# Value rows on every fourth partition, and key transposes that write columns four apart, in a fused attention and feed-forward kernel

## The chip, the cores and the metric

The kernel runs on one core of a Trainium2 chip. The metric is the device time of one execution in microseconds (us); each kernel was run several times, and the median is quoted. The profiled execution has a "span" that is about 2 to 3 us shorter than its time (271.4 us beside times of 274.21 to 275.49 before). PE is the matmul engine, DVE the vector engine, ACT the scalar engine, POOL the general engine (here it casts fp32 to bf16), and SP issues DMA.

## The reference, cut to what matters

```python
def _attn_ref(q, k, v, p):           # q, k, v: (8, 8, 576, 64); p: (8, 8, 32, 64), all * 0.1
    p_packed = sm_attn(p, k, v)      # 32 queries against 576 keys, per batch and head
    return sm_attn(q, p_packed, p_packed)

def _moe_ref(x, w_in, w_out):        # x: the attention output as (4608, 512), w_in: (512, 2048), w_out: (2048, 512)
    h = np.maximum(x @ w_in, 0.0)
    return (h * h) @ w_out
```

The first softmax sums over all 576 keys of a head, so the keys may be handled in any order, as long as a key's score and its value meet on the same partition of the second matmul.

## The kernel before

A key index is `a*18 + j`, with `a` from 0 to 31 and `j` from 0 to 17. Keys are loaded with (head, `a`) on the 128 partitions. The kernel has DVE transpose 32x32 blocks (32 keys by 32 of the head dimension in `tr_k`), so that `kT` holds the head dimension on partitions and keys as columns. A chunk of 128 columns becomes the stationary operand of a score matmul, so **column c of a chunk becomes partition c of the scores**, and the value of that key has to lie on partition c of the value tile. Before, columns run (`jp`, `a`), so a value load with fixed `jp` fills 32 adjacent partitions.

```python
def dma_v(self, i, h0, h1, eng):                       # six loads per batch
    src = v[self.b, h0:h1].rearrange("h (a j) d -> a h j d", j=JT)
    if i < 4:
        eng.dma_start(v_f[32 * i:32 * i + 32, h0:h1, :GM * D].rearrange("p h (g d) -> p h g d", d=D),
                      src[:, :, i * GM:(i + 1) * GM, :])
    else:
        o = 32 * (i - 4)
        eng.dma_start(v_f[o:o + 32, h0:h1, GM * D:], src[:, :, JM + i - 4, :])

def tr_k(self, qd):
    nc.vector.transpose(                               # 1024 elements per partition
        self.kT[:, qd, :, :GM * P].rearrange("p dh (g jp a) -> p jp g dh a", jp=4, a=32), ...)
    nc.vector.transpose(                               # the remaining 64 keys: 128 elements
        self.kT[:, qd, :, GM * P:].rearrange("p dh (j a) -> p j dh a", a=32), ...)

def s1(self, qd):                                      # scores: kT is the stationary operand
    ...
    nc.tensor.matmul(ps[:, g * P:(g + 1) * P], lhsT=self.kT[:, qd, dh, g * P:(g + 1) * P],
                     rhs=pT_bd[self.b % 2][:, ...], start=(dh == 0), stop=(dh == 1))
```

The order of the instructions on each engine is not written by hand. While the kernel is built, a greedy planner places every step on a model time line, with a cost in us for each, and the program is emitted in that order. A cost that is changed changes the order:

```python
def load_step(name, us, fn, slot): ...
load_step(f"Lv.{b}.{p}.{i}", (1.22 if i < 4 else 0.37) / n, ...)   # value loads: 5.6 us a batch
us = 1.45 if nm == "k" else 1.38                                    # key and query transposes
# ... some 20 streams of such steps, then plan.run()
```

The softmax here doesn't subtract the row's maximum and nothing guards it: scores larger than these inputs give would overflow.

Of the kernel before, what the change touches and what calls it, by code (L numbers as in the profile page):

```python
# [9 lines left out]
ACT = mybir.ActivationFunctionType  # L10
ALU = mybir.AluOpType
F32 = mybir.dt.float32
BF16 = mybir.dt.bfloat16

P = 128
D = 64
NP = 32
QH = 4
JT = 18
GM = 4  # L20
REM = 64
FB = 128
WCH = 512

# [262 lines left out]
def kernel_impl(tc, q, k, v, p, w_in, w_out, out):  # L287
    nc = tc.nc
    B, H, S, Dh = q.shape
    assert Dh == D and S == JT * 32 and H == 2 * QH  # L290
    NQD = H // QH
# [6 lines left out]
    JH = JT // 2  # L298
    TOK = B * S
    NW = 6  # L300
    JM = JT // GM * GM
    NT = TOK // P

    with ExitStack() as ctx:
        ctx.enter_context(tc.manual_schedule())
        consts = ctx.enter_context(tc.tile_pool(name="consts", bufs=1))
# [3 lines left out]
        att = ctx.enter_context(tc.tile_pool(name="att", bufs=2))  # L310
# [10 lines left out]
        w_in_b = consts.tile([P, QH, DFF], BF16, name="w_in_b")  # L321
        w_out_b = consts.tile([P, NFB, NE], BF16, name="w_out_b")
        ones_bd = consts.tile([P, P], BF16, name="ones_bd")
        ones_c = consts.tile([P, 2], BF16, name="ones_c")
        e1_r = [consts.tile([P, NQD, P], BF16, name=f"e1_r{i}") for i in range(2)]
        idle_b = consts.tile([P, 256], BF16, name="idle_b")
        v_f = consts.tile([P, H, (GM + 1) * D], F32, name="v_f")
        pT = consts.tile([P, B * NQD, 2, 32], BF16, name="pT")
# [13 lines left out]
                eng.tensor_copy(dst, src)  # L342

        def setup():
            nc.vector.memset(pT_bd[0][:, :512], 0.0)
            nc.vector.memset(ones_c, 8.0)
            nc.vector.memset(ones_c[REM:, 1:2], 0.0)
            for i in range(2):
                nc.gpsimd.memset(e1_r[i][REM:], 0.0)
            nc.vector.memset(v_f[64:128, :, GM * D:], 0.0)  # L350
            for i in range(2):
                nc.gpsimd.memset(pq_bd[i][:, :512], 0.0)
            nc.gpsimd.memset(idle_b, 0.0)
            nc.gpsimd.memset(ones_bd, 0.0)
            for h in range(QH):
                nc.gpsimd.memset(ones_bd[32 * h:32 * h + 32, 32 * h:32 * h + 32], 0.125)
            nc.gpsimd.memset(pT_bd[1][:, :512], 0.0)

        def keep_clock(ps):
            for _ in range(plan.fill):  # L360
                nc.tensor.matmul(ps, lhsT=idle_b[:, :P], rhs=idle_b, start=True, stop=True)
# [23 lines left out]
        class Loads:  # L385
# [9 lines left out]
                getattr(self, name)[qd] = f  # L395

            def dma_v(self, i, h0, h1, eng):
                src = v[self.b, h0:h1].rearrange("h (a j) d -> a h j d", j=JT)
                if i < 4:
                    eng.dma_start(v_f[32 * i:32 * i + 32, h0:h1, :GM * D].rearrange("p h (g d) -> p h g d", d=D),  # L400
                                  src[:, :, i * GM:(i + 1) * GM, :])
                else:
                    o = 32 * (i - 4)
                    eng.dma_start(v_f[o:o + 32, h0:h1, GM * D:], src[:, :, JM + i - 4, :])

            def new_kq(self, name, qd):
                getattr(self, name + "b")[qd] = qkv.tile([P, JT * D], BF16, name=name + "_b", tag="kqb")
# [34 lines left out]
        class Att:  # L442
# [14 lines left out]
                    self.t.qb[qd][:].rearrange("p (j dh dl) -> p j dh dl", dh=2, dl=32))  # L457

            def tr_k(self, qd):
                self.tile_of("kT", att, [P, NQD, 2, S], BF16, bufs=1)  # L460
                nc.vector.transpose(  # L461
                    self.kT[:, qd, :, :GM * P].rearrange("p dh (g jp a) -> p jp g dh a", jp=4, a=32),
                    self.t.kb[qd][:, :JM * D].rearrange("p (jp g dh dl) -> p jp g dh dl", jp=4, dh=2, dl=32))
                nc.vector.transpose(
                    self.kT[:, qd, :, GM * P:].rearrange("p dh (j a) -> p j dh a", a=32),
                    self.t.kb[qd][:, JM * D:].rearrange("p (j dh dl) -> p j dh dl", dh=2, dl=32))

            def s1(self, qd):
                ps = ps_att.tile([P, 512], F32, name="ps_a", tag="a")
                keep_clock(ps[:, :256])  # L470
                for g in range(GM):
                    for dh in range(2):
                        nc.tensor.matmul(ps[:, g * P:(g + 1) * P], lhsT=self.kT[:, qd, dh, g * P:(g + 1) * P],  # L473
                                         rhs=pT_bd[self.b % 2][:, (qd * 2 + dh) * P:(qd * 2 + dh + 1) * P],
                                         start=(dh == 0), stop=(dh == 1))
                self.ps1[qd] = ps
# [5 lines left out]
            def s1_rest(self):  # L482
                ps = ps_att.tile([P, 512], F32, name="ps_a", tag="a")
                keep_clock(ps[:, :256])
                for qd in range(NQD):
                    for dh in range(2):
                        nc.tensor.matmul(ps[:REM, qd * P:(qd + 1) * P], lhsT=self.kT[:, qd, dh, GM * P:],  # L487
                                         rhs=pT_bd[self.b % 2][:, (qd * 2 + dh) * P:(qd * 2 + dh + 1) * P],
                                         start=(dh == 0), stop=(dh == 1))
                self.psr = ps  # L490

            def s1_rest_exp(self):
                nc.scalar.activation(e1_r[self.b % 2][:REM], self.psr[:REM, :NQD * P], ACT.Exp, scale=0.125)

            def pv(self, qd):
                if qd == 0:
                    self.ps_pp = ps_att.tile([P, 512], F32, name="ps_pp", tag="a")
                    keep_clock(self.ps_pp[:, :256])
                ps = self.ps_pp
                def e1(g, i0, i1):  # L500
                    return self.e1[:, qd, g, i0:i1] if g < GM else e1_r[self.b % 2][:, qd, i0:i1]

                for pr in range(2):
                    h0 = qd * QH + 2 * pr
                    c0 = qd * P + pr * 64
                    for g in range(GM + 1):
                        nc.tensor.matmul(ps[:, c0:c0 + 64], lhsT=self.t.v[:, g, h0 * D:(h0 + 2) * D],  # L507
                                         rhs=e1(g, pr * 64, pr * 64 + 64), start=(g == 0), stop=(g == GM))
                for g in range(GM + 1):
                    o = 1 if g == GM else 0  # L510
                    nc.tensor.matmul(ps[:, 256 + qd:257 + qd], lhsT=e1(g, 0, P), rhs=ones_c[:, o:o + 1],  # L511
                                     start=(g == 0), stop=(g == GM))
# [149 lines left out]
        def stage(*pieces):  # L662
            return list(pieces)

        def load_step(name, us, fn, slot):
            return Step(name, [stage([("SP", 0.45, fn)]), stage([("DMA", us, lambda: None)])], (), slot, (), lag=1.4)

        def load_steps(b):
            def kq(nm, qd):
                return load_step(f"L{nm}.{b}.{qd}", 1.5, lambda: L[b].dma_kq(nm, qd), [("kq", 1)])  # L670

            def vv(p, n):
                h0, h1 = p * H // n, (p + 1) * H // n
                return [load_step(f"Lv.{b}.{p}.{i}", (1.22 if i < 4 else 0.37) / n,
                                  lambda i=i: L[b].dma_v(i, h0, h1, nc.sync), [("v", 1)] if p == 0 and i == 0 else [])
                        for i in range(6)]

            if b == 0:
                return [kq("k", 0), kq("k", 1), kq("q", 0)] + vv(0, 2) + vv(1, 2) + [kq("q", 1)]
            return [kq("k", 0), kq("k", 1)] + vv(0, 1) + [kq("q", 0), kq("q", 1)]  # L680
# [16 lines left out]
        def cast_steps(b, nm, engs):  # L697
            res = []
            halves = 2 if b == 0 else 1
            for qd in QDS:  # L700
                if nm == "v":
                    lands = [f"Lv.{b}.{qd if b == 0 else 0}.{j}" for j in range(6)]
                    us, fn, new = 1280 / halves, L[b].cast_v, f"Bv.{b}.0"
                    if qd == 0:
                        res.append(Step(new, [stage([("-", 0.0, L[b].new_v)])], lands, [("vb", 1)]))
                else:
                    lands = [f"L{nm}.{b}.{qd}"]
                    us, new = 1152 / halves, f"B{nm}.{b}.{qd}"
                    res.append(Step(new, [stage([("-", 0.0, lambda qd=qd: L[b].new_kq(nm, qd))])], lands, [("kqb", 1)]))

                    def fn(qd, i, n, e):
                        L[b].cast_kq(nm, qd, i, n, e)

                piece = [cast_alt(us, engs, lambda e, fn=fn, qd=qd, i=i: fn(qd, i, halves, e)) for i in range(halves)]
                give = [("kq", 1, lands[0])] if nm != "v" else [("v", 1, f"Lv.{b}.0.0")] if qd == NQD - 1 else []
                res.append(Step(f"C{nm}.{b}.{qd}", [stage([("-", 0.0, lambda: None)]), piece], [new] + lands, (), give))
            return res
# [121 lines left out]
        for nm in "kvq":  # L839
            plan.stream(5, sum([cast_steps(b, nm, (A, V, Q) if b == 0 else (Q,)) for b in range(B)], []))  # L840
# [53 lines left out]
```

## Time and profile before

| | before |
|---|---|
| time, median of the first three runs | 274.54 us (274.21 to 275.49) |
| PE busy | 243.0 of 271.4 us |
| PE idle before 75 us | 22.3 us |
| key transposes per head group (4 of the 8 heads) | 1235 + 269 ns |
| rate while values are loaded | about 205 GB/s |

From the page of the kernel before: busy us per engine, then busy tenths in 40 slices of 6.8 us; the row PEclk is the clock granted to PE in tenths, DMA the busy share of the DMA engines.

```profile
span 271.4 us, 5108 instructions
...
PE 243.0 (90%) x1840; PEld 135.4 (50%) x1840; DVE 172.7 (64%) x325; ACT 168.6 (62%) x302; POOL 82.7 (30%) x127
...
PE   0436967999989999999999999999999999999992
...
DVE  4756799999949899859768974976266504510000
...
PEclk9999999999999999999999999999999999999997
DMA  7999999999897999807955911111111131113223
```

PE is short of work only in the first slices, while the DMA row is full. Busy us of each engine in three stretches (after the stretch and its length: PE, PE weight loads, DVE, ACT, POOL, then granted clock, DMA share and GB/s):

```profile
core 0: us, PE busy (x) PEld busy (x) DVE busy (x) ACT busy (x) POOL busy (x), PEclk, DMA share, GB/s
0.00:75.00 75.00, 52.69 (x387) 29.03 (x388) 60.83 (x106) 42.17 (x73) 38.42 (x56) 1.00 1.02 300
75.00:100.00 25.00, 24.01 (x237) 13.46 (x236) 19.86 (x40) 17.77 (x37) 18.79 (x39) 1.00 0.94 275
100.00:250.00 150.00, 149.78 (x1148) 85.56 (x1141) 91.99 (x181) 105.76 (x188) 25.47 (x34) 1.00 0.40 107
...
```

PE lacks 75.00 - 52.69 = 22.3 us in the first stretch, 1.0 in the second and nothing worth naming up to 250 us. The chain of waits, followed back from the last instruction (start, duration, what):

```profile
...
3.62 7.74 DMA v_f<-in_v_dram
...
11.37 3.08 DMA v_f<-in_v_dram
...
21.96 10.57 DMA kq_f<-in_k_dram
...
```

It begins with 10.8 us of value loads, and the keys of batch 1 are waited for at 21.96 us. The DMA rate in the first 16 us, in slices of 0.4 us:

```profile
DMA  0000779999999969999999999999999899989997
GB/s 0 0 0 0 127 196 380 390 378 226 440 415 415 369 265 392 415 373 314 179 159 200 244 195 210 228 199 200 205 239 175 135 284 347 346 328 319 238 210 200
```

By 7.2 us, 1.9 MB have come in (keys, queries and packed queries, but for the first few values), from 4 us on mostly at 370 to 440 GB/s. The values follow; from 7.6 to 12.8 us the rate is 135 to 244 GB/s, although the busy row shows 8 or 9. Then the next loads push it up again. The key transposes, in the groups of instructions (busy us and mean ns of one behind the first bar):

```profile
...
L461 DVE STREAM_TRANSPOSE kT<-k_b 128x1024 bf16<-128x1024 bf16 x16 | 19.8, 1235 | 5.7 <-PE ps_a L487 4.8 <-POOL k_b L342 0.6
L464 DVE STREAM_TRANSPOSE kT<-k_b 128x128 bf16<-128x128 bf16 x16 | 4.3, 269 | 0.0
...
```

### The profile page before, as it was taken

What the parts mean: (1) busy time and instruction counts of PE and PEld (TensorE: products, weight loads), DVE (VectorE), ACT (ScalarE), POOL (GpSimd) and SP (SyncE); (2) the same over time, 40 slices, a digit from 0 to 9 for tenths busy, and PEclk for the clock granted to TensorE, in tenths of its full rate; (3) what the DMA queues carried; (4) which work ended last, traced back from release to release, by engine and by line L of the source; (5) the groups of instructions that cost most, each with busy time, mean ns of one, the idle gap of its engine ahead of it and who ended that gap; (6) DMA issues with size and microseconds to landing.
All of it is one profiled execution on the core that took longest, in us unless ns stands there. A gap on an engine that the chain in (4) does not pass through costs nothing.

```text
span 271.4 us, 5108 instructions
## 1 busy us (share of the span) xinstructions
PE 243.0 (90%) x1840; PEld 135.4 (50%) x1840; DVE 172.7 (64%) x325; ACT 168.6 (62%) x302; POOL 82.7 (30%) x127
## 2 busy tenths in 40 slices
PE   0436967999989999999999999999999999999992
PEld 0322443456555544665565466556546646644441
DVE  4756799999949899859768974976266504510000
ACT  3436646867548798788868975976587717821110
POOL 5432338629589381362246213000000000000000
PEclk9999999999999999999999999999999999999997
DMA  7999999999897999807955911111111131113223
GB/s 258 230 310 398 270 319 386 358 261 334 176 291 236 259 330 239 332 1 168 328 173 119 280 41 40 41 39 42 39 41 39 39 77 41 40 50 76 73 74 77
DMA packets 31129, 46.99 MB, mean 173 GB/s; under 512 B 10113, under 2 KB 18305, under 8 KB 31105
## 3 DMA queue, kind: packets, MB, share of 16 engines
q1 hardware_dynamic: 30576, 46.55, 60.5%
q8 instruction: 14, 0.23, 0.4%
q10 hardware_dynamic: 528, 0.13, 0.2%
q14 instruction: 11, 0.08, 0.1%
HBM read 37.22 MB, written 9.44 MB: 172 GB/s over the span
## 4 chain that ended last, share of the span: by engine, by line
PE 60%; DVE 18%; DMA 11%; SPq 4%; ACT 2%; issue 2%; POOL 1%; DVEq 0%; POOLq 0%; ACTq 0%
PE ps_o L636 31%; PE ps_h L612 17%; DVE gT L627 6%; DMA v_f<-in_v_dram 4%; DMA kq_f<-in_k_dram 4%; DMA out_dram<-o_sb 3%; DVE qT L455 3%; PE ps_a L542 3%; PE ps_s L572 3%; SPq L645 3%; PE ps_a L473 2%; DVE a L600 2%; PE ps_pp L507 2%; DVE M L552 2%; ACT o_sb L340 1%
## 5 line engine op out<-in xcount | busy, mean ns | idle before, releaser
L636 PE MATMUL ps_o<-w_out_b,gT 128*128 128x512 bf16 x576 | 147.5, 379 | 0.4 <-DVE w_out_b L342 0.3
L620 ACT ACTIVATE r<-ps_h 128x576 bf16<-128x576 f32 x124 | 78.2, 651 | 26.6 <-PE ps_h L612 18.9
L627 DVE TENSOR_TENSOR gT<-r 128x576 bf16<-128x576 bf16 x128 | 71.1, 580 | 28.6 <-ACT r L620 27.7
L612 PE MATMUL ps_h<-a,M 128*128 128x288 bf16 x512 | 82.1, 292 | 2.2 <-DVE r L622 1.2
L636 PEld LDWEIGHTS <-gT 128*128 128x128 bf16 x576 | 54.6, 98 | 50.2 <-issue 4.4
L612 PEld LDWEIGHTS <-M 128*128 128x128 bf16 x512 | 49.7, 99 | 31.6 <-issue 6.1
L340 ACT COPY o_sb<-ps_o 128x512 f32<-128x512 f32 x29 | 17.0, 585 | 32.5 <-DMA out_dram<-o_sb 25.8
L550 ACT ACTIVATE M<-ps_a,rD 128x512 bf16<-128x512 f32 x39 | 26.4, 686 | 6.2 <-PE ps_a L542 5.8
L342 POOL CAST q_b<-kq_f 128x1152 bf16<-128x1152 f32 (+1 forms) x16 | 19.7, 1244 | 25.5 <-DMA kq_f<-in_q_dram 25.2
L342 POOL CAST v_b<-v_f 128x1280 bf16<-128x1280 f32 (+1 forms) x15 | 18.8, 1279 | 27.1 <-PE ps_pp L511 10.1
L461 DVE STREAM_TRANSPOSE kT<-k_b 128x1024 bf16<-128x1024 bf16 x16 | 19.8, 1235 | 5.7 <-PE ps_a L487 4.8
L342 POOL CAST k_b<-kq_f 128x1152 bf16<-128x1152 f32 (+1 forms) x15 | 17.7, 1180 | 13.5 <-DMA kq_f<-in_k_dram 9.4
L455 DVE STREAM_TRANSPOSE qT<-q_b 128x1152 bf16<-128x1152 bf16 x16 | 21.4, 1358 | 0.4 <-ACT q_b L340 0.4
L552 DVE TENSOR_SCALAR M<-ps_a,rD 128x512 bf16<-128x512 f32 x25 | 18.7, 747 | 4.4 <-PE ps_a L542 4.2
L473 PE MATMUL ps_a<-pT_bd,kT 128*128 128x128 bf16 x128 | 10.0, 230 | 11.0 <-DVE pT_bd L342 8.3
L542 PE MATMUL ps_a<-w_in_b,ppT 64*32 64x512 bf16 x256 | 16.8, 413 | 3.0 <-ACT M L550 1.1
L342 POOL COPY pT_bd<-pT 32x64 bf16<-32x64 bf16 x56 | 13.5, 267 | 10.9 <-PE ps_a L487 8.8
L473 PEld LDWEIGHTS <-kT 128*128 128x128 bf16 x128 | 8.6, 103 | 13.4 <-DVE kT L461 9.2
L579 ACT ACTIVATE e<-ps_s,rD 128x576 bf16<-128x576 f32 x16 | 11.4, 739 | 5.8 <-PE ps_s L572 5.7
L342 DVE CAST pq_bd<-ps_pp 32x64 bf16<-32x64 f32 x32 | 7.0, 218 | 11.2 <-PE ps_pp L511 5.9
L572 PE MATMUL ps_s<-qT,pq_bd 128*128 128x288 bf16 x64 | 11.0, 306 | 3.1 <-ACT pq_bd L340 1.8
L600 DVE TENSOR_TENSOR a<-e,rs 128x576 bf16<-128x576 bf16 x16 | 13.6, 848 | 0.0
(51 smaller groups left out, 145.0 us busy)
## 6 DMA issues: line engine op xcount, KB each, us to landing
kq_f<-in_k_dram SPq DMA_DIRECT2D x16, 576.0 KB, 8.2
kq_f<-in_q_dram SPq DMA_DIRECT2D x16, 576.0 KB, 7.1
out_dram<-o_sb SPq DMA_DIRECT2D x144, 64.0 KB, 1.7
v_f<-in_v_dram SPq DMA_DIRECT2D x28, 256.0 KB, 5.9
w_f<-in_moe_w_in_dram SPq DMA_DIRECT2D x8, 512.0 KB, 8.2
w_f<-in_moe_w_out_dram SPq DMA_DIRECT2D x8, 512.0 KB, 8.4
v_f<-in_v_dram SPq DMA_DIRECT2D x8, 128.0 KB, 6.7
v_f<-in_v_dram SPq DMA_DIRECT2D x14, 64.0 KB, 5.9
```

What stands on the lines that cost most here:

```text
L340: nc.scalar.copy(dst, src)
L342: eng.tensor_copy(dst, src)
L455: nc.vector.transpose(self.qT[:, qd].rearrange("p dh (j a) -> p j dh a", a=32), self.t.qb[qd][:].rearrange("p (j dh dl) -> p j dh dl", dh= ...
L461: nc.vector.transpose(self.kT[:, qd, :, :GM * P].rearrange("p dh (g jp a) -> p jp g dh a", jp=4, a=32), self.t.kb[qd][:, :JM * D].rearrang ...
L473: nc.tensor.matmul(ps[:, g * P:(g + 1) * P], lhsT=self.kT[:, qd, dh, g * P:(g + 1) * P], rhs=pT_bd[self.b % 2][:, (qd * 2 + dh) * P:(qd * ...
L542: nc.tensor.matmul(pss[qd][o:o + 32, :], lhsT=self.ppT[64 * e:64 * e + 64, qd, pr, :], rhs=w_in_b[64 * e:64 * e + 64, qd * 2 + pr, c * WCH ...
L550: nc.scalar.activation(dst, self.psm[c][e], ACT.Copy, scale=self.rD[:, e:e + 1])
L552: nc.vector.tensor_scalar_mul(dst, self.psm[c][e], self.rD[:, e:e + 1])
L612: nc.tensor.matmul(ps[:, c, :HALF], lhsT=a.M[:, qd, fb * FB:(fb + 1) * FB], rhs=a.a2[:, qd, c * HALF:(c + 1) * HALF], start=(qd == 0), sto ...
L620: nc.scalar.activation(dst, src, ACT.Relu)
L627: eng.tensor_tensor(out=gT[:, fb, o:o + S], in0=r, in1=r, op=ALU.mult)
L636: nc.tensor.matmul(po[t], lhsT=gT[:, fb, n0:n0 + P], rhs=w_out_b[:, fb, :], start=(fb == 0), stop=(fb == NFB - 1))
```

## The change

The intent is to load the values faster, by letting each value load of 32 partitions reach over the whole height of the tile; the loads into 32 neighbours came in at 135 to 244 GB/s. Value load `i` now writes partitions `i, i+4, i+8, ...`, so key columns must run (`a`, `jp`) too: a transpose writes its 32 columns four apart. Keys are divided 5, 5, 4, 4 among the four loads, with rows of 1.25 and 1 KB, and the fifth chunk is padded with zeros. The planner is told that a batch of values takes 3.24 us instead of 5.6.

```diff
 def dma_v(self, i, h0, h1, eng):
-    src = v[self.b, h0:h1].rearrange("h (a j) d -> a h j d", j=JT)
-    ... # four loads into v_f[32*i:32*i+32], two of 256-byte rows
+    n = GM + 1 if i < 2 else GM
+    src = v[self.b, h0:h1].rearrange("h (a j) d -> a h (j d)", j=JT)
+    eng.dma_start(v_f[i:P:4, h0:h1, :n * D], src[:, :, J0[i] * D:(J0[i] + n) * D])   # J0 = (0, 5, 10, 14)
 def tr_k(self, qd):
-    ... "p dh (g jp a) -> p jp g dh a" ...
+    for i, n in (0, GM + 1), (2, GM):
+        nc.vector.transpose(
+            kT[:, qd, :, :n * P].rearrange("p dh (g a jp) -> p jp g dh a", jp=4, a=32)[:, i:i + 2], ...)
 # score matmul of the fifth chunk: 128 rows instead of 64 (zeros in kT, v_f and ones_c)
-    return [load_step(..., (1.22 if i < 4 else 0.37) / n, ...) for i in range(6)]
+    return [load_step(..., (0.9 if i < 2 else 0.72) / n, ...) for i in range(4)]
 # cut: memsets of the padding, the exp of the fifth chunk over 128 partitions
```

More of the change, by code (lines that the diff above doesn't have):

```diff
@@ L20 @@
 GM = 4
-REM = 64
+J0 = (0, 5, 10, 14)
 FB = 128
@@ L300, in kernel_impl @@
     NW = 6
-    JM = JT // GM * GM
     NT = TOK // P
@@ L323, in kernel_impl @@
         ones_bd = consts.tile([P, P], BF16, name="ones_bd")
-        ones_c = consts.tile([P, 2], BF16, name="ones_c")
-        e1_r = [consts.tile([P, NQD, P], BF16, name=f"e1_r{i}") for i in range(2)]
+        ones_c = consts.tile([P, 33], BF16, name="ones_c")
+        msk = consts.tile([P, 32], BF16, name="msk")
+        kT = consts.tile([P, NQD, 2, (GM + 1) * P], BF16, name="kT")
         idle_b = consts.tile([P, 256], BF16, name="idle_b")
@@ L344, in setup @@
         def setup():
+            nc.vector.memset(v_f[:, :, GM * D:], 0.0)
             nc.vector.memset(pT_bd[0][:, :512], 0.0)
-            nc.vector.memset(ones_c, 8.0)
-            nc.vector.memset(ones_c[REM:, 1:2], 0.0)
-            for i in range(2):
-                nc.gpsimd.memset(e1_r[i][REM:], 0.0)
-            nc.vector.memset(v_f[64:128, :, GM * D:], 0.0)
+            nc.vector.memset(ones_c[:, :1], 8.0)
+            nc.vector.memset(msk, 0.0)
+            nc.vector.memset(msk[:].rearrange("p (x y) -> p x y", y=4)[:, :, :2], 8.0)
+            nc.vector.transpose(ones_c[:, 1:33], msk)
+            for qd in range(NQD):
+                nc.gpsimd.memset(kT[:, qd, :, GM * P:], 0.0)
             for i in range(2):
@@ L397, in dma_v @@
             def dma_v(self, i, h0, h1, eng):
-                src = v[self.b, h0:h1].rearrange("h (a j) d -> a h j d", j=JT)
-                if i < 4:
-                    eng.dma_start(v_f[32 * i:32 * i + 32, h0:h1, :GM * D].rearrange("p h (g d) -> p h g d", d=D),
-                                  src[:, :, i * GM:(i + 1) * GM, :])
-                else:
-                    o = 32 * (i - 4)
-                    eng.dma_start(v_f[o:o + 32, h0:h1, GM * D:], src[:, :, JM + i - 4, :])
+                n = GM + 1 if i < 2 else GM
+                src = v[self.b, h0:h1].rearrange("h (a j) d -> a h (j d)", j=JT)
+                eng.dma_start(v_f[i:P:4, h0:h1, :n * D], src[:, :, J0[i] * D:(J0[i] + n) * D])
             def new_kq(self, name, qd):
@@ L459, in tr_k @@
             def tr_k(self, qd):
-                self.tile_of("kT", att, [P, NQD, 2, S], BF16, bufs=1)
-                nc.vector.transpose(
-                    self.kT[:, qd, :, :GM * P].rearrange("p dh (g jp a) -> p jp g dh a", jp=4, a=32),
-                    self.t.kb[qd][:, :JM * D].rearrange("p (jp g dh dl) -> p jp g dh dl", jp=4, dh=2, dl=32))
-                nc.vector.transpose(
-                    self.kT[:, qd, :, GM * P:].rearrange("p dh (j a) -> p j dh a", a=32),
-                    self.t.kb[qd][:, JM * D:].rearrange("p (j dh dl) -> p j dh dl", dh=2, dl=32))
+                for i, n in (0, GM + 1), (2, GM):
+                    nc.vector.transpose(
+                        kT[:, qd, :, :n * P].rearrange("p dh (g a jp) -> p jp g dh a", jp=4, a=32)[:, i:i + 2],
+                        self.t.kb[qd][:, J0[i] * D:(J0[i] + 2 * n) * D].rearrange(
+                            "p (jp g dh dl) -> p jp g dh dl", jp=2, dh=2, dl=32))
             def s1(self, qd):
@@ L472, in s1 @@
                     for dh in range(2):
-                        nc.tensor.matmul(ps[:, g * P:(g + 1) * P], lhsT=self.kT[:, qd, dh, g * P:(g + 1) * P],
+                        nc.tensor.matmul(ps[:, g * P:(g + 1) * P], lhsT=kT[:, qd, dh, g * P:(g + 1) * P],
                                          rhs=pT_bd[self.b % 2][:, (qd * 2 + dh) * P:(qd * 2 + dh + 1) * P],
@@ L486, in s1_rest @@
                     for dh in range(2):
-                        nc.tensor.matmul(ps[:REM, qd * P:(qd + 1) * P], lhsT=self.kT[:, qd, dh, GM * P:],
+                        nc.tensor.matmul(ps[:, qd * P:(qd + 1) * P], lhsT=kT[:, qd, dh, GM * P:],
                                          rhs=pT_bd[self.b % 2][:, (qd * 2 + dh) * P:(qd * 2 + dh + 1) * P],
@@ L492, in s1_rest_exp @@
             def s1_rest_exp(self):
-                nc.scalar.activation(e1_r[self.b % 2][:REM], self.psr[:REM, :NQD * P], ACT.Exp, scale=0.125)
+                self.tile_of("e1r", att, [P, NQD, P], BF16)
+                nc.scalar.activation(self.e1r, self.psr[:, :NQD * P], ACT.Exp, scale=0.125)
             def pv(self, qd):
@@ L500, in e1 @@
                 def e1(g, i0, i1):
-                    return self.e1[:, qd, g, i0:i1] if g < GM else e1_r[self.b % 2][:, qd, i0:i1]
+                    return self.e1[:, qd, g, i0:i1] if g < GM else self.e1r[:, qd, i0:i1]
                 for pr in range(2):
@@ L673, in vv @@
                 h0, h1 = p * H // n, (p + 1) * H // n
-                return [load_step(f"Lv.{b}.{p}.{i}", (1.22 if i < 4 else 0.37) / n,
+                return [load_step(f"Lv.{b}.{p}.{i}", (0.9 if i < 2 else 0.72) / n,
                                   lambda i=i: L[b].dma_v(i, h0, h1, nc.sync), [("v", 1)] if p == 0 and i == 0 else [])
-                        for i in range(6)]
+                        for i in range(4)]
             if b == 0:
@@ L701, in cast_steps @@
                 if nm == "v":
-                    lands = [f"Lv.{b}.{qd if b == 0 else 0}.{j}" for j in range(6)]
+                    lands = [f"Lv.{b}.{qd if b == 0 else 0}.{j}" for j in range(4)]
                     us, fn, new = 1280 / halves, L[b].cast_v, f"Bv.{b}.0"
```

## The prediction

> **What bounds the kernel now.** TensorE, once fed. Windows view: PE is idle 28.4 of 271.4 us, 22.3 of that before 75 us, 4.4 in the last output stores. From 100 to 250 us it is always busy, and counting matmuls there at their shortest times (0.216 us for 128x512, 0.122 for 128x288) fills nearly all of it: fixed work. Time can be won only at the start. There the DMA row stands at 90 to 110% until 100 us. The chain of waits starts with 10.8 us of value loads (3.62 to 14.45), then batch 1's keys (21.96 to 32.5), then DVE work (90 to 100% busy from 30 to 75 us).
>
> **The suspected cost: loads into 32 adjacent partitions.** In fine slices of the GB/s row, key/query and weight loads move 380 to 420 GB/s, value loads only 180 to 240: about 7.2 to 12.7 us for batch 0 (1.18 MB), again 30 to 36.5 us for batch 1. [...]
>
> **Removed.** Six value loads per batch become four (batch 0: 12 become 8); 4096 rows of 256 B go. Estimated from those rates, 1.18 MB at 205 GB/s = 5.7 us becomes 3.0 to 3.6 us at 330 to 390: 2 to 2.7 us per batch, about 19 us of DMA time over eight. [...]
>
> **Added.** Key transposes: 1235 + 269 ns become 640 + 512 elements. From these durations, slope 1.08 ns per element and 131 ns fixed, an estimate of 822 + 684 = 1506 ns: unchanged if writing columns 8 bytes apart is free; at half rate 1.2 us more for each of 16. The remainder's scores get 128 rows instead of 64, same matmul count; its exp stays near 374 ns. Setup gains under 1 us, hidden behind the first loads.
>
> **On the critical path.** Batch 0's values land 2 to 2.5 us earlier and carry the start (PV, w_in, batch 1's keys at 32.5) with them. Batches 1 and 2 give 2 to 2.5 us of DMA time each, but DVE is full from 36 to 75 us, so only part returns: earlier w_out for the first ps_o (about 7 us of PE capacity is lost from 30 to 45 us), and batch 2's start at 76 us, whose chain waited on POOL 4.3 us for v_f at 61. From batch 3 on the saving is hidden. Sum: 2.3 + about 1.6 = 3.9 us. The instruction order is replanned with cheaper loads: 1 us either way.
>
> **Predicted: 270.6 us, 8 in 10 within 266.8 to 273.8. Faster by over 2%: 0.28; within 2%: 0.69; slower: 0.03.**
>
> **Signs.** Right: over 320 GB/s during value loads; batch-0 value casts end near 13 us instead of 15.1; the first ps_h matmul near 25 us instead of 27.4; PE idle before 75 us down by 3 to 4 us; transposes of 0.82 and 0.68 us; 100 to 250 us unchanged in shape. Wrong: value rate still near 210; transposes of 1.2 us or more; DVE from 36 to 75 us swallowing all of the shift.
>
> **What would make it wrong.** Above 274: slower strided transposes. Below 267: the load rate, not DVE, governed everything up to 75 us, so that the savings of batches 0 to 2 add up.

The step from 205 to between 330 and 390 GB/s stands as the estimate, beside the 380 to 420 that the other loads moved in the trace of before. The sum came to 2.3 + about 1.6 = 3.9 us, and 274.5 less 3.9 gives the 270.6 predicted.

## The result, and the profile after

The changed kernel takes 287.62 us (median of four runs, 285.49 to 289.06), the kernel before 274.38 us in the runs beside it. The ratio is 1.0512, with a 95% interval of 1.0437 to 1.0587: **5% slower**. A ratio here is from fast runs alone, so it is not quite the ratio of the quoted medians.

The same views of the kernel after:

```profile
span 283.6 us, 5045 instructions
...
PE 242.1 (85%) x1809; PEld 137.9 (49%) x1840; DVE 186.1 (66%) x325; ACT 171.2 (60%) x305; POOL 80.7 (28%) x126
...
PE   0368568948996989998997999899999999999993
...
DVE  4968997998599899789869955985255522520000
...
PEclk9999987997999999999999999999999999999999
DMA  7999999923884929719615711201121112112222
```

```profile
core 0: us, PE busy (x) PEld busy (x) DVE busy (x) ACT busy (x) POOL busy (x), PEclk, DMA share, GB/s
0.00:75.00 75.00, 48.24 (x346) 27.62 (x350) 62.16 (x101) 39.49 (x70) 38.93 (x61) 0.93 0.85 297
75.00:100.00 25.00, 21.73 (x228) 13.63 (x230) 21.45 (x41) 19.10 (x39) 11.67 (x22) 1.00 0.79 259
100.00:250.00 150.00, 143.55 (x1110) 83.72 (x1129) 101.78 (x184) 106.86 (x189) 30.12 (x45) 1.00 0.34 106
...
```

PE idle time before 75 us did not fall; it rose from 22.3 to 26.8 us, and the next stretches lose 3.3 and 6.5 us as well. (Of the 6.5 us, 4.7 are four waits of about 1 us, at 102.5, 128.6, 152.6 and 181.9 us. The rest are gaps shorter than 0.25 us, and may be records that are missing: the page lists 1809 matmuls, but 1840 weight loads.) DVE has 13.4 us more work in all (186.1 against 172.7): by the two pages the key transposes take 19.6 us more (43.7 against 19.8 + 4.3), and the multiplications that write `gT` 4.6 us less (66.5 against 71.1). The clock row dips in slices 6, 7 and 10. The start of the chain of waits:

```profile
...
5.86 2.69 DVE kT L459 x2
...
9.46 1.38 DVE kT L459
...
10.87 1.34 DVE kT L459
...
12.26 1.05 PE ps_a L469 x8
...
```

The value loads have left the chain, as was hoped. Key transposes have taken their place at once: 2.69 + 1.38 + 1.34 us of them before the second score matmuls at 12.26. The DMA rate in the first 16 us:

```profile
DMA  0000598699999989999999999999899999899999
GB/s 0 0 0 0 161 392 323 228 350 264 461 429 403 415 357 415 398 377 369 369 357 364 357 366 360 324 315 333 323 332 289 210 227 225 292 394 410 405 374 384
```

This is the success of the change. The values, from about 6.8 to 10.4 us, come in at 324 to 377 GB/s instead of 135 to 244. The change also makes rows and loads fewer, but packets of the same 1,024 bytes took 83 ns on average in the trace before and 55 ns in the trace after, so the rate does not come from larger rows alone. The first matmul of `ps_h` (the feed-forward part) starts at 24.26 us instead of 27.37. But the lead is gone soon after: the first `ps_o` matmul (the last product of the feed-forward part) starts at 45.14 us (45.33 before), and the scores of batch 2 at 76.07 us (75.79 before). The key transposes:

```profile
...
L459 DVE STREAM_TRANSPOSE kT<-k_b 128x640 bf16<-128x640 bf16 x16 | 25.8, 1611 | 5.2 <-PE ps_a L483 5.0
L459 DVE STREAM_TRANSPOSE kT<-k_b 128x512 bf16<-128x512 bf16 x16 | 21.4, 1336 | 0.0
...
```

They take 1611 + 1336 = 2947 ns in place of 1504 (the records of a pair overlap by about 0.2 us, so that a pair keeps DVE busy for about 2.75 us). And in PE's time line there are idle stretches that the kernel before does not have (the last bracket: us idle, and what ended it):

```profile
...
43.30 0.39 PE L539 MATMUL ps_a<-w_in_b,ppT 64*32 64x512 bf16 x1 [2.71 <-DVE ppT L342]
63.63 0.39 PE L633 MATMUL ps_o<-w_out_b,gT 128*128 128x512 bf16 x1 [3.00 <-DVE gT L624]
...
```

The longest idle stretch of the kernel before between 21 and 110 us is 1.31 us.

### The profile page after: what moved, and what is told of

Same layout as the page of the kernel before. It is cut to its first block, busy times and chain, and to the rows that moved or that the text cites. A ratio compares the mean times of both kernels' runs of the same rounds, so it can differ in the third digit from the quotient of the medians.

```text
span 283.6 us, 5045 instructions
## 1 busy us (share of the span) xinstructions
PE 242.1 (85%) x1809; PEld 137.9 (49%) x1840; DVE 186.1 (66%) x325; ACT 171.2 (60%) x305; POOL 80.7 (28%) x126
## 4 chain that ended last, share of the span: by engine, by line
PE 56%; DVE 21%; ACT 6%; DMA 6%; issue 4%; SPq 3%; POOL 3%; ACTq 0%; POOLq 0%
PE ps_o L633 27%; PE ps_h L609 19%; DVE kT L459 11%; DMA out_dram<-o_sb 4%; SPq L642 3%; PE ps_a L539 3%; PE ps_a L469 2%; ACT o_sb L340 2%; DVE M L549 2%; DVE pq_bd L342 2%; DVE gT L624 1%; DMA w_f<-in_p_dram 1%; ACT r L617 1%; PE ps_s L569 1%; PE ps_pp L504 1%
## 5 line engine op out<-in xcount | busy, mean ns | idle before, releaser
L633 PE MATMUL ps_o<-w_out_b,gT 128*128 128x512 bf16 x545 | 141.0, 382 | 4.9 <-DVE gT L624 3.9
L617 ACT ACTIVATE r<-ps_h 128x576 bf16<-128x576 f32 x126 | 79.8, 651 | 28.8 <-PE ps_h L609 20.8
L624 DVE TENSOR_TENSOR gT<-r 128x576 bf16<-128x576 bf16 x128 | 66.5, 539 | 37.4 <-ACT r L617 36.1
L609 PE MATMUL ps_h<-a,M 128*128 128x288 bf16 x512 | 84.9, 298 | 2.4 <-DVE a L597 1.3
L609 PEld LDWEIGHTS <-M 128*128 128x128 bf16 x512 | 50.9, 101 | 31.6 <-issue 5.2
L459 DVE STREAM_TRANSPOSE kT<-k_b 128x640 bf16<-128x640 bf16 (+1 forms) x32 | 43.7, 1473 | 5.2 <-PE ps_a L483 5.0
L547 ACT ACTIVATE M<-ps_a,rD 128x512 bf16<-128x512 f32 x38 | 25.4, 684 | 9.0 <-PE ps_a L539 8.8
L342 POOL CAST q_b<-kq_f 128x1152 bf16<-128x1152 f32 x14 | 17.9, 1287 | 32.9 <-DMA kq_f<-in_q_dram 20.1
L342 POOL CAST k_b<-kq_f 128x1152 bf16<-128x1152 f32 (+1 forms) x15 | 16.7, 1120 | 18.8 <-DMA kq_f<-in_k_dram 8.0
L476 ACT ACTIVATE e<-ps_a 128x512 bf16<-128x512 f32 x16 | 8.9, 597 | 11.9 <-PE ps_a L469 11.8
L539 PEld LDWEIGHTS <-ppT 64*32 64x32 bf16 x256 | 4.6, 90 | 23.1 <-issue 16.7
```

Source lines behind the costliest of these rows:

```text
L342: eng.tensor_copy(dst, src)
L459: nc.vector.transpose(kT[:, qd, :, :n * P].rearrange("p dh (g a jp) -> p jp g dh a", jp=4, a=32)[:, i:i + 2], self.t.kb[qd][:, J0[i] * D:( ...
L539: nc.tensor.matmul(pss[qd][o:o + 32, :], lhsT=self.ppT[64 * e:64 * e + 64, qd, pr, :], rhs=w_in_b[64 * e:64 * e + 64, qd * 2 + pr, c * WCH ...
L547: nc.scalar.activation(dst, self.psm[c][e], ACT.Copy, scale=self.rD[:, e:e + 1])
L609: nc.tensor.matmul(ps[:, c, :HALF], lhsT=a.M[:, qd, fb * FB:(fb + 1) * FB], rhs=a.a2[:, qd, c * HALF:(c + 1) * HALF], start=(qd == 0), sto ...
L617: nc.scalar.activation(dst, src, ACT.Relu)
```

## The experiments

Three suspects came out of the two traces: the strided transposes (T), the new instruction order (R1), and the fast loads themselves, by contention or by the clock (R2). Some experiments pair keys with the wrong values. They all passed the comparison with the reference, so **that comparison does not see a wrong pairing here**. The inputs are scaled by 0.1, so the softmax is nearly uniform; that this is the reason is argued, not shown.

### 1. Strided transposes alone, in the old order (e2_before_strided)

```diff
-    self.kT[...].rearrange("p dh (g jp a) -> p jp g dh a", jp=4, a=32),
+    self.kT[...].rearrange("p dh (g a jp) -> p jp g dh a", jp=4, a=32),
```

The instruction lists of all engines are the same as before. 

> The kernel before, in its own instruction order, with only the main key transposes (1024 elements) writing columns four apart; wrong result on purpose. Theory T (strided transpose writes are the loss): each such transpose takes about 2.4 us instead of 1.235, 16 times, DVE busy up by about 19 us, and the time rises to 283 to 289 us. Rival R1 (the new instruction order is what costs) and rival R2 (the faster loads collide with something, or the granted clock falls by itself): 274 to 276 us, as before.

Measured: 282.05 us beside 274.98, ratio 1.0253 (1.0209 to 1.0296). The group line:

```profile
...
L461 DVE STREAM_TRANSPOSE kT<-k_b 128x1024 bf16<-128x1024 bf16 x16 | 39.3, 2455 | 5.1 <-PE ps_a L487 4.5 <-POOL k_b L342 0.3
...
```

So T is at work by itself: 1235 ns became 2455, and the run became 2.5% slower, just below the range expected. But 5.1% is not explained by this alone.

### 2. The kernel after with contiguous transposes (e5_after_contiguous)

```diff
-    kT[...].rearrange("p dh (g a jp) -> p jp g dh a", jp=4, a=32)[:, i:i + 2],
+    kT[...].rearrange("p dh (g jp a) -> p jp g dh a", jp=4, a=32)[:, i:i + 2],
```

Same order as after, wrong pairing. 

> The kernel after, same instruction order on all engines, key transposes writing 32 contiguous columns again; wrong result on purpose. Theory T: transposes of about 0.82 and 0.69 us, no clock dip from 30 to 50 us, time 267 to 272 us (the gain that was predicted from the loads). R1 and R2: it stays at 282 to 288 us.

Measured: 278.32 us, ratio 1.0124 (1.0059 to 1.0188). The transposes took 834 + 669 ns, and the time fell by 9 us, yet it stayed above the kernel before, although the loads were fast and the transposes cheap. Neither theory fits alone: T predicted at most 272, R1 and R2 at least 282. Its first two stretches, and idle stretches of PE:

```profile
...
0.00:75.00 75.00, 51.69 (x375) 28.72 (x380) 58.50 (x104) 42.03 (x74) 41.50 (x66) 0.93 0.87 302
75.00:100.00 25.00, 21.11 (x197) 12.95 (x199) 18.45 (x36) 17.06 (x34) 13.29 (x24) 0.86 0.74 262
...
```

```profile
...
37.86 2.08 PE L609 MATMUL ps_h<-a,M 128*128 128x288 bf16 x8 [1.72 <-DVE r L619]
41.82 1.22 PE L539 MATMUL ps_a<-w_in_b,ppT 64*32 64x512 bf16 x8 [1.89 <-DVE ppT L342]
87.33 0.75 PE L539 MATMUL ps_a<-w_in_b,ppT 64*32 64x512 bf16 x8 [2.57 <-DVE gT L624]
...
```

The clock dips and the gaps before 100 us did not go away with the strided writes. The four waits after 100 us did: this trace has no PE gap above 0.25 us from 100 to 250 us.

### 3. The planner told the truth about transposes (e3_after_told)

```diff
-    us = 1.45 if nm == "k" else 1.38
+    us = 2.95 if nm == "k" else 1.38
```

> The kernel after, with the planner told that the key transposes of one group take 2.95 us instead of 1.45, so that it orders the work around them; correct result. If the loss is mostly that the order was planned for the wrong duration (R1): 276 us or less. If it is the DVE time itself (T): 279 to 286 us.

Measured: 277.11 us, ratio 1.0071 (1.0023 to 1.0119). The work is that of the change, the result is correct, and 10 us of the loss are gone; it falls between the two forecasts. The order therefore matters as much as the DVE time does.

### 4. The new load cost in the planner alone (e4_before_plan_only)

```diff
-    load_step(..., (1.22 if i < 4 else 0.37) / n, ...)
+    load_step(..., (0.70 if i < 4 else 0.22) / n, ...)
```

Loads and transposes are those of before. 

> The kernel before with nothing but the planner's cost of value loads lowered to the new total (3.2 us instead of 5.6 per batch); loads and transposes as before, correct result. T: 273 to 277 us, only the noise of another order. R1 (an order planned for faster loads is bad): 280 us or more.

Measured: 280.98 us, ratio 1.0194 (1.0135 to 1.0253). A number in the planner, with no work changed, cost 6 us. R1 is real.

### 5. Fast loads in the old order, without and with strides (e6_order_before_contig, e7_order_before_strided)

To take the order out of the comparison, the planner keeps six value steps at the old costs, and the last two issue nothing. The lists of PE, DVE, ACT and POOL then agree with those of before except for the shapes and the memsets of the change itself.

```diff
 def dma_v(self, i, h0, h1, eng):
+    if i > 3:
+        return
-    load_step(..., (0.9 if i < 2 else 0.72) / n, ...) for i in range(4)
+    load_step(..., (1.22 if i < 4 else 0.37) / n, ...) for i in range(6)
```

e7 is the whole change in this order; e6 has contiguous transposes as well (wrong pairing).

> Fast value loads alone: the four new loads, contiguous transposes, and the instruction order of the kernel before (the planner keeps six load steps at the old costs; the last two issue nothing). Keys and values are paired wrongly on purpose. If the predicted gain from the loads exists (2 to 4 us) and the new order hid it: 270.5 to 273 us. If faster loads gain nothing or collide with other work (R2): 274.5 us or more.

> The whole change, correct, in the instruction order of the kernel before. If the loss of the change is the sum of strided transposes (7.1 us in that order) and of the new order: e6 plus 6 to 8 us, 277 to 281 us. If the order is innocent and the parts only interact: 285 us or more, as after.

Measured for e6: ratio 0.9688 (0.9649 to 0.9728). Its six runs fall into two groups, 265.35 to 266.85 and 269.75 to 271.64; the second lies over 1.5% above the fastest run and is left out of the ratio. All six have a median of 268.3, beside 274.8, a gain of 2.4%; so the gain is 2.4 to 3.1%, by whether the second group counts. For e7: 280.54 us, ratio 1.0222 (1.0193 to 1.0250), all six within 1.5 us. The first two stretches of e6:

```profile
...
0.00:75.00 75.00, 55.20 (x450) 31.71 (x451) 60.62 (x112) 43.99 (x80) 42.55 (x76) 1.00 0.96 338
75.00:100.00 25.00, 25.00 (x225) 13.49 (x223) 23.52 (x45) 20.87 (x40) 15.84 (x21) 1.00 0.82 274
...
```

And the first and third of e7:

```profile
...
0.00:75.00 75.00, 50.05 (x369) 28.08 (x370) 65.54 (x106) 40.91 (x71) 36.55 (x53) 0.98 0.87 303
...
100.00:250.00 150.00, 146.04 (x1139) 84.48 (x1139) 102.71 (x186) 107.75 (x191) 25.87 (x35) 1.00 0.34 105
...
```

In e6 PE lacks 19.8 us in the first stretch instead of 22.3, nothing in the second, and the clock reads 1.00. (Over the whole span idle time falls by 3.9 us; the other 3.7 of the 7.6 us between the two profiled spans are PE busy time, 239.3 against 243.0 us for the same matmuls. Why they took less was not found.) Batch 2's scores start at 70.57 us instead of 75.79. So the fast loads do gain, and more than was forecast; R2 falls. In this order the strides turn a gain of 3.1% into a loss of 2.2%: in e7 PE lacks 25.0 us in the first stretch and 4.0 in the third.

### 6. What a column step costs (e8_strides)

The transpose of 512 elements was given another column step in each pair of batches.

```diff
+    if s == 1:  o = d.rearrange("p dh (jp g a) -> p jp g dh a", jp=4, a=32)[:, 2:4]
+    elif s == 2: o = d.rearrange("p dh (g a jp) -> p jp g dh a", jp=2, a=32)[:, :, 4:8]
+    elif s == 8: ...   # s = 4 in batches 0 and 1 as in the change; 16 in batch 7
```

> The second key transpose (512 elements) with a column step of 4 in batches 0 and 1, 1 in 2 and 3, 2 in 4 and 5, 8 in 6 and 16 in 7; wrong result on purpose, only durations count. Theory S1[...]: 0.67 us at step 1 and the same 1.33 us at 2, 4, 8 and 16. Theory S2[...]: step 2 close to 0.67 us, step 4 1.33, steps 8 and 16 above 1.33.

The single run took 291.06 us, which says nothing here. From DVE's time line, one transpose each of step 1, 2, 8 and 16:

```profile
...
61.74 0.71 DVE L475 STREAM_TRANSPOSE kT<-k_b 128x512 bf16<-128x512 bf16 x1
...
122.98 0.75 DVE L475 STREAM_TRANSPOSE kT<-k_b 128x512 bf16<-128x512 bf16 x1
...
145.72 2.47 DVE L475 STREAM_TRANSPOSE kT<-k_b 128x512 bf16<-128x512 bf16 x1 [1.19 <-PE ps_a L487]
...
177.91 2.37 DVE L475 STREAM_TRANSPOSE kT<-k_b 128x512 bf16<-128x512 bf16 x1 [1.43 <-PE ps_a L487]
...
```

Step 4 took 1.34 us in the kernel after. So: 0.71, 0.75, 1.34, 2.47 and 2.37 us for steps of 1, 2, 4, 8 and 16 elements of two bytes. S1 is wrong: step 2 is nearly free. S2, by which the cost grows with the step, is right up to step 8; 16 cost no more than 8. Step 4 took 1.9 times as long as step 1, step 8 took 3.5 times; step 3 was not tried. Why, no run shows.

### 7. Two queues for the value loads (e9_two_queues)

```diff
-    L[b].dma_v(i, h0, h1, nc.sync)
+    L[b].dma_v(i, h0, h1, nc.scalar if i in (2, 3, 5) else nc.sync)
```

> The kernel before with value loads 2, 3 and 5 (partitions 64 to 127, and 32 to 63 of the remainder) issued by ACT instead of SP, so that the loads of the two partition halves may run side by side; transposes contiguous, correct. [...]over 300 GB/s during value loads and 270 to 274 us. If ACT waits for free buffers and issue time eat it: 275 us or more.

Measured: 275.93 us, ratio 1.0093 (1.0034 to 1.0152). In slices of 0.5 us the rate was 174 to 340 GB/s while values came in, against 135 to 244 (in slices of 0.4 us) in before. Interleaving the halves from two queues raised the rate somewhat, and did not make the run faster.

### 8. How much an order is worth by itself (e10_before_nudged, e11_before_nudged_load, e13_after_contig_nudged, e14_order_told_old_loads)

```diff
 # e10, on before                          # e13, on e5: the same two numbers
-    us = 1.45 if nm == "k" else 1.38
+    us = 1.50 if nm == "k" else 1.36
 # e11, on before: (1.22 -> 1.25 if i < 4 else 0.37) / n
 # e14, on e7 (the whole change): us = 2.95 if nm == "k" else 1.36
```

> The kernel before, same work, with the planner's key and query transpose costs nudged by 0.05 and 0.02 us (to what the trace shows, 1.50 and 1.36), which gives another instruction order. If the order of before is a tuned one and any replanning loses several us: 278 to 283 us. If only the lowered load cost made the bad order: 273 to 276 us.

> The kernel before, same work, with the planner's cost of one value load nudged from 1.22 to 1.25 us; the order changes in few places on PE and DVE. Tuned-order theory: between 275 and 280 us. Otherwise 273 to 276 us.

> Fast value loads and contiguous transposes (pairing wrong on purpose), planned with the lowered load costs as in after, but with transposes nudged to 1.50 and 1.36 us: a third order for the same work (e5 took 278 us, e6 268). If the lowered load cost makes bad orders: 276 to 280 us again. If the order is a matter of chance of a greedy planner: 266 to 274 us.

> The whole change, correct, planned with the true transpose cost (2.95 us) and the old load costs; the counterpart of e3 (277 us with the new load costs) and e7 (280.5 us with the old transpose cost). If the planner's knowledge of the transposes is what helps: 272 to 278 us. If not: 279 us or more. Under no order is it expected below 270 us, since the DVE work stays.

Measured: e10 272.82 us (ratio 0.9885, 0.9821 to 0.9949), e11 274.45 (0.9939, 0.9884 to 0.9995), e13 277.8 (1.0125, 1.0075 to 1.0175), e14 278.72 (1.0151, 1.0105 to 1.0197).

The idea that the order of before is a finely tuned one that any nudge spoils is wrong: two nudges gave slightly faster orders. But e13 repeats e5: all three orders planned with the lowered load cost for transposes of about 1.5 us (e4, e5, e13) lose against the ones planned with the old cost. In their traces PE waits for DVE in the middle of the start-up, as in the lines of e5 (in e4 for POOL and ACT too: 3.07 us at 41 us, 2.51 us at 75 us). Which of the planner's other costs makes the true load cost harmful was not found and stays open. e14 beside e3 suggests that with the transposes at their true cost the load cost makes little difference (278.7 and 277.1; the two also differ in the cost of query transposes, 1.36 and 1.38), and no order of the change ran faster than before.

### 9. Less transpose work with the old loads (e12_pair_transposes, e12b_pair_transposes, e15_pairs_told)

Two neighbouring values of one key can be moved as one 4-byte element, so that a transpose has half as many elements. Score weights are then read two elements apart; the packed queries are transposed in the same way, so that both sides match. The loads are those of before.

```diff
+    kf = self.t.kb[qd][:].bitcast(F32)
+    o = self.kT[:, qd].rearrange("p s e -> p (s e)").bitcast(F32)
-    lhsT=self.kT[:, qd, dh, g * P:(g + 1) * P]
+    lhsT=self.kT[:, qd, g * P:(g + 1) * P, dh]
 # e15 also: us = 0.90 if nm == "k" else 1.36
```

> The kernel before with its loads and its order, key transposes on pairs of bf16 as one 4-byte element (half as many elements, written side by side), score matmuls reading weights two elements apart; correct pairing. If DVE time at the start is what the run is sensitive to (e2: 19.5 us of DVE more cost 7 us): transposes of about 0.67 and 0.20 us, DVE time down by about 10 us, 270 to 273 us. If the weight loads get slow at step 2 or DVE time below the present does not matter: 274 us or more.

> The same kernel as in the run of pair transposes that was unclear, five rounds: 271 to 275 us if about 10 us less DVE work helps, 275 to 277 us if not.

> Pair transposes with the planner told their true cost (0.90 and 1.36 us), the loads of before, correct pairing: the version that the experiments point to. 268 to 273 us if the shorter DVE work and a fitting order add up; 275 us or more if the order falls badly.

Measured: e12 276.82 us, with runs from 271.85 to 279.96; again with five rounds, e12b: 275.29 us, ratio 1.0026 (0.9970 to 1.0081); e15 274.5 us, ratio 0.9999 (0.9944 to 1.0054). The main transpose in e12:

```profile
...
L463 DVE STREAM_TRANSPOSE kT<-k_b 128x512 f32<-128x512 f32 x16 | 11.2, 702 | 7.3 <-PE ps_a L489 4.8 <-POOL k_b L342 2.2
...
```

The transposes took 702 + 202 ns, 600 ns less, and the weight loads stayed at 103 ns, as before. It gained nothing (ratios 1.0026 and 0.9999). With the slow loads, DVE time below the present is not what these two runs waited for. This would fit the fact that strides cost 7 us on slow loads (e2 against before) and 12 to 15 us on fast ones (e7 against e6, with and without e6's slower group): the slow loads would hide part of the cost. That is argued, not shown, and the two differences are not quite alike: e2 strides the large transpose alone (1.2 us more per head group), e7 both (1.4 us more).

### 10. Fast loads, correct pairing, no slow write (e16_key_pairs, e17_key_pairs_nudged)

A way that fails first: contiguous `kT`, with the score matmul reading its weights in the order (`a`, `jp`). It is refused before it runs: the build stops at that matmul, with the message that the stationary operand must be a pattern "with exactly one free dimension".

e8 and e12 suggest another. The cast of the keys, which POOL does anyway, writes the keys of `jp` = 0 and 1 (and of 2 and 3) side by side. The transpose then moves such a pair of keys as one 4-byte element. It has half as many elements, and columns come out in the order of the change.

```diff
 def cast_kq(...):                                  # keys only
+    cast(eng, d[qd][:, o:o + w].rearrange("p (g d e) -> p e g d", e=2, d=D),
+         self.k[qd][:, o:o + w].rearrange("p (e g d) -> p e g d", e=2, d=D))
 def tr_k(self, qd):
+    kf, o = self.t.kb[qd][:].bitcast(F32), kT[:, qd].bitcast(F32)
+    for y, n in (0, GM + 1), (1, GM):
+        nc.vector.transpose(o[:, :, :n * 64].rearrange("p dh (g a y) -> p y g dh a", a=32, y=2)[:, y],
+            kf[:, J0[2 * y] * 32:(J0[2 * y] + 2 * n) * 32].rearrange("p (g dh dl) -> p g dh dl", dh=2, dl=32))
 # e16: planner as in e7; e17: transposes planned at 1.50 and 1.36 us
```

The pairing was checked index by index outside the chip: each of the 36,864 entries of one head's `kT` belongs to the key whose value lies on that column's partition and chunk.

> Fast value loads, in the order of before, with correct pairing: the key cast writes two keys side by side, and the transpose moves such a pair as one 4-byte element, so that it has half as many elements, each 8 bytes from the next. From the step run (2.15 ns per element at 8 bytes): 0.92 and 0.79 us for the two transposes, 1.71 in all, against 1.50 before and 2.95 in the change. If the strided transposes were what ate the gain of the loads: 265 to 271 us, as in the run with fast loads and contiguous transposes. If something else in the pairing of fast loads with column step four does it, or the key cast gets slow by its step of two: 274 us or more.

> The same with the planner's transpose costs nudged to 1.50 and 1.36 us, the nudge that gave the kernel before 272.8 us. Another order for the same work: 264 to 273 us; over 275 would say that the order alone undoes the gain here too.

Measured: **e16 265.74 us (264.37 to 267.06), ratio 0.9696 (0.9645 to 0.9747)**; e17 271.34 us, ratio 0.9883 (0.9835 to 0.9931). The transposes:

```profile
...
L470 DVE STREAM_TRANSPOSE kT<-k_b 128x320 f32<-128x320 f32 x16 | 8.0, 502 | 4.3 <-PE ps_a L494 4.0
L470 DVE STREAM_TRANSPOSE kT<-k_b 128x256 f32<-128x256 f32 x16 | 6.5, 404 | 0.2 <-POOL k_b L342 0.2
...
```

They take 502 + 404 ns; the 0.92 and 0.79 expected from bytes between elements are wrong. 4-byte elements 8 bytes apart went about as fast as adjacent ones: e12's two sizes of adjacent ones, 702 and 202 ns for 512 and 64 elements, give an estimate of 488 and 416 ns for these. 2-byte elements 8 bytes apart took twice the time of adjacent ones (2.15 against 1.08 ns per element). What sets the pace was not found: no run was made to tell a rule in bytes from one in elements. The key cast on POOL got slower, 989 + 882 ns in place of 1217, and that did not show in the time. The first two stretches:

```profile
...
0.00:75.00 75.00, 56.19 (x453) 32.29 (x458) 59.34 (x115) 45.13 (x81) 47.44 (x83) 1.00 0.94 329
75.00:100.00 25.00, 24.55 (x222) 13.21 (x224) 22.40 (x44) 21.05 (x40) 17.89 (x25) 1.00 0.90 305
...
```

PE lacks 18.8 us in the first stretch, and the clock reads 1.00. So with the strides made harmless, the gain of the loads is there with correct pairing. This version beats both kernels; e17 shows that the order alone can take 5.6 us of it away.

## Why the prediction was wrong, point by point

With fast loads, four runs form a square of order and transposes. In the old order: -3.1% with contiguous transposes (e6), +2.2% with strided ones (e7). In the new order: +1.2% (e5) and +5.1% (after). So the strides cost 5.3 points in the old order and 3.9 in the new one; the new order costs 4.4 points with contiguous transposes and 2.9 with strided ones. Both causes are there in every row and column, and together they cost less than their sum. On the way from before over e6 and e7 to after, with 274.5 us as 100%, the steps are -3.1, +5.3 and +2.9 points, or about -8.6, +14.7 and +8 us. That these add up to the measured loss follows from the way they are taken, and confirms nothing. If all runs of e6 count, the first two are about -6.5 and +12 us.

- **The bound.** Right for the kernel before: the work from 100 to 250 us is fixed, and time can be won only at the start and held while PE stays fed. In e6 and before, PE is busy for 150.0 and 149.8 of these 150 us. In after it is not (143.55; up to 1.7 us of what is missing may be missing records): the four waits of about 1 us are there with the strides and gone without them in the same order (e5), so later batches pay for the strides too.
- **The suspected cost, and "Removed".** Right. The rate while values load went from about 205 to between 324 and 377 GB/s, inside the forecast 330 to 390 in all but one of its slices of 0.4 us. Why loads into 32 adjacent partitions are slow was not shown; that the spread ones are fast is measured. The first `ps_h` matmul came at 24.26 us; "near 25" was forecast.
- **"Added": the step that failed first.** The prediction put the transposes at "822 + 684 = 1506 ns: unchanged if writing columns 8 bytes apart is free", and counted them as free. They took 1611 + 1336 ns. From the two sizes the slope is (1611 - 1336)/128 = 2.15 ns per element, twice the 1.08 of contiguous columns. The "1.2 us more for each of 16" of the condition was close to the truth (1.44), and "What would make it wrong" put "slower strided transposes" first, so the alternative was known and costed; it was given too small a weight, on no run that could tell.
- **"The instruction order is replanned ...: 1 us either way": the second step that failed.** It was 8 us here, 10 to 12 us between e5 and e6 with the same work (with and without e6's slower group), and 6 us in e4 where nothing but the plan differs.
- **"On the critical path", "Sum: 2.3 + about 1.6 = 3.9 us": mis-sized.** The loads are worth 8.6 us in the old order with cheap transposes (e6; 6.5 if all its runs count). The prediction held that a full DVE would swallow most of what batches 1 and 2 save. The clause "the load rate, not DVE, governed everything up to 75 us" was nearer to it: e12b and e15 took 600 ns off each pair of transposes under the slow loads and gained nothing. But e2 shows that more DVE time than before does cost, under slow loads too.
- **The clock, not foreseen.** In after the granted clock was 0.83 from 30 to 50 us and 0.89 from 60 to 75. It fell to half three times, for 3.4 us each, from 34.1, 44.3 and 64.8 us on; PE had been idle for 1.95, 2.71 and 3.00 us at a stretch up to 34.3, 43.3 and 63.6 us. `ps_h` matmuls from 34.1 to 37.5 us follow each other at 240 ns instead of 123. In e7 it fell to half for 3.4 us from 35.9 us on, at a gap of 1.95 us that ended at 36.1 us; in e5 for 6.8 us from 89.0 us on, after one of 2.57 us that ended at 87.3 us. In two traces the matmuls show it: in e10, 12 `ps_h` matmuls took 2.51 us from 41.62 us on, after a gap of 1.70 us that ended at 39.1 us, and in e17 8 of them took 2.41 us from 57.86 us on, after one of 1.57 us that ended at 54.3 us; 8 took 1.15 us in e10 at 34.71 us. In before, e6 and e16, whose longest gaps between 30 and 110 us are 1.31, 1.18 and 1.07 us, the clock reads 1.00 up to 100 us. (Its first record is at 33 us in before and at 31 us in after. The row shows 9 earlier too, although 12 `ps_h` matmuls from 30.55 us on took 2.86 us in before.) So in these traces a wait of PE came with slower matmuls, and with a cost above its own length. A rule for when the clock falls is not shown. What the clock alone cost in all was not separated.

## What to carry to other kernels

A layout that speeds up a load has a second end, where something else must write or read the same permutation: measure that end by itself, for each step, before adding up the gain. When a planner or scheduler orders the instructions, compare a change in a fixed order too, since the reordering that comes along can be larger than the change (here 10 to 12 us between e5 and e6, against 6.5 to 8.6 for the loads). And if the fast layout needs a scattered write, look for a wider element: here the cast that ran anyway put two keys side by side, and the same columns then cost 0.9 us instead of 2.9.
